# Pairing the third output tile of the six-block groups across groups, in an attention-and-MLP kernel with a written-out order

## The chip, the cores and the metric

The kernel runs on one core of one Trainium2 chip. The time is device microseconds from one launch of the whole program, the median of several runs. A core has TensorE (PE in the profile, with its weight loads as PEld), VectorE (DVE), ScalarE (ACT), GpSimd (POOL) and SyncE (SP), which here only issues DMAs. Each engine works through its own queue in order.

## The reference

Squared-ReLU attention, then an MLP with the quick GELU. Eight batches, 12 heads, 448 rows, head width 64; the MLP is 768 to 2048 to 768 on 3584 rows.

```python
scores = np.matmul(q, k.transpose(0, 1, 3, 2)) / np.sqrt(64)
attn = np.maximum(scores, 0.0) ** 2 / 448
x = np.matmul(attn, v).transpose(0, 2, 1, 3).reshape(8 * 448, 768)
h = x @ w_in
out = (h / (1.0 + np.exp(-1.702 * h))) @ w_out
```

All arrays are float32 in DRAM; the kernel multiplies in float16 and accumulates in float32.

## The kernel before, in words

**Attention** goes by units: a unit is four heads of one batch, 24 in all (three to a batch). k and q of a unit are loaded (by SP as float32 and cast on an engine, or by a POOL DMA that casts on the way), transposed (on PE for units 0 to 5, by a DMA on SP for the others), and multiplied in 7 steps of scores (line 150). Each step leaves two PSUM banks; relu (lines 161 and 163, on DVE or ACT) evicts each into an `at` tile, and square (L169 on ACT, or the helper tt, L88, on DVE or POOL) squares the tile in place. attn_v (L181) multiplies all seven `at` tiles of the unit with v, and xt_evac brings the result into `xe` or `xo`, the transposed input of the MLP.

**The MLP** goes by groups of 64-row blocks: `gblk = [6, 8] * 4`, so even groups have 384 rows and odd groups 512. Its first product is done for group 0 and half of group 1 plainly (m1, L228, word f), and for all others by Strassen's scheme in Winograd's form with seven products in place of eight (unit_product, word u, on weight differences winS and input differences T). The gelu on ACT goes into a `gf` tile of float32 (five buffers), and a "widening" on POOL (L217) scales it to float16 and writes it to the group's `ge` or `go` tile. Four words make up a unit's outputs there: t (snapshot of a PSUM bank), b (DVE adds the other bank to it), g (gelu), v (widening).

**The second product** (gelu times w_out, 768 columns in two halves of 384) goes by output tiles of 128 rows. An odd group has four such tiles, an even group three. Two tiles of a group (m and m+1) make a pair: seven products (pair_product, word p, eight matmuls each; L203 is the matmul helper that all of these share) on four sums of the gelu tile (a_sum, word A, DVE, tiles `as0` and `as1`, or in place) and on four differences of w_out (w_sum, word W). PSUM is evicted by h, l (L81, L85 and L396). An even group's third tile has no partner: in group 0 all three tiles are multiplied plainly (m2, word m, 16 matmuls for each half, evicted by n), in groups 2, 4 and 6 the third tile goes through single (word i, also 16 matmuls for each half, with one sum, n == 5).

**What sets the order.** The whole program is one list of words in a string. Each word is a function with its arguments, the engine after a colon and the PSUM banks after an at-sign: `s0.3@4.5` is scores of unit 0, step 3, into banks 4 and 5; `x0.3:p` squares on POOL; `p1.0.2` is product 2 of the pair (0, 1) of group 1. They are issued in this order, and every engine takes its own in it. The list was written by a planner that is not part of the kernel. A tile pool with n buffers makes the (n+1)th tile wait until an earlier one has been read.

Words used later: Lk, Lq (SP load), jk, jq (POOL load with cast), K, Q (cast), tk, tq (transpose on PE), ek, eq (its eviction), V (load of v), jwa, jwb (half of a w_in block), jo (a w_out block), S, T, W (Strassen differences of w_in, of the input, of w_out), z (dummy matmuls), o and q (stores, L328 and L334).

The start of the order before:

```python
"Lk0 z13@0 jk1 V1 jq1 I V0 K0:d tk0@1 z1 ek0 jk2 Lq0 Q0:a tq0@2 eq0 tk1@3 s0.3@4.5 "
```

Of the kernel before, what the change touches and what calls it, by code (L numbers as in the profile page):

```python
# [15 lines left out]
def kernel(  # L16
# [35 lines left out]
    for name, bufs in (("cst", 1), ("kst", 1), ("qst", 1), ("k16", 2), ("q16", 2), ("v16", 4),  # L52
                       ("kT", 3), ("qT", 3), ("at", 11), ("xe", 1), ("xo", 2),
                       ("T1", 1), ("T2", 1), ("T4", 1), ("ge", 1), ("go", 1), ("gf", 5),
                       ("as0", 1), ("as1", 1), ("osb", 3)):
        pool(name, bufs)
# [151 lines left out]
    def gt_of(g):  # L208
        if g not in gts:
            gts[g] = new("ge" if g % 2 == 0 else "go", [128, NF, 64 * gblk[g]], F16)  # L210
        return gts[g]

# [25 lines left out]
    def m1_widen(e, p, g, f):  # L238
        n = 64 * gblk[g]
        widen(e, gt_of(g)[:, f, 0:n], gfs.pop((g, f))[:, 0:n])  # L240
# [66 lines left out]
    def unit_widen(e, p, g, i, n):  # L307
        fh, th = unit_place[n]
        hn = 32 * gblk[g]
        f = WQ * i + 2 * fh  # L310
        widen(e, gt_of(g)[:, f:f + 2, th * hn:(th + 1) * hn],
              half_of(gfs.pop((g, i, unit_tile[n])), g).rearrange("p (t c) -> p t c", t=2))
# [9 lines left out]

    def store(e, p, g, m):
        t = osb.pop((g, m))
        for i in range(2):
            b, j = divmod(gcum[g] + 2 * m + i, J)
            r0 = b * S + j
            nc.sync.dma_start(out=out[r0:r0 + 63 * J + 1:J, :], in_=t[64 * i:64 * i + 64, :])  # L328

    def store_part(e, p, g, m, h, i):  # L330
        b, j = divmod(gcum[g] + 2 * m + i, J)
        r0 = b * S + j
        c = slice(h * NOUT, (h + 1) * NOUT)
        (nc.scalar if e == "a" else nc.sync).dma_start(  # L334
            out=out[r0:r0 + 63 * J + 1:J, c], in_=osb[g, m][64 * i:64 * i + 64, c])

    def m2(e, p, g, m, h):
        op[g, m, h] = bank(p, "op")
        mm(op[g, m, h][:, 0:NOUT], lambda f: gts[g][:, f, m * 128:(m + 1) * 128],
           lambda f: wout[h][f // WO][:, f % WO, :], NF, True)  # L340

    def m2_out(e, p, g, m, h):
        copy(e, out_tile(g, m)[:, h * NOUT:(h + 1) * NOUT], op.pop((g, m, h))[:, 0:NOUT], 1.0 / SC)
# [8 lines left out]
    def part(g, m, i):  # L352
        return gts[g][:, i * HF:(i + 1) * HF, m * 128:(m + 1) * 128]
# [3 lines left out]
    def a_sum(e, p, g, m, n):  # L357
        a11, a12 = part(g, m, 0), part(g, m, 1)
        if n == 5:
            sums[g, m, 5] = new(f"as{p.pop(0)}", [128, HF, 128], F16, "asum")  # L360
            tt(sums[g, m, 5], a11, a12, ALU.add, e)
            return
# [36 lines left out]
    def single(e, p, g, m, h):  # L399
        op[g, m, h] = bank(p, "os")  # L400
        o = op[g, m, h][:, 0:NOUT]
        a1, a2 = part(g, m, 0), part(g, m, 1)
        s, t = ((a1, wout[0][0]), (a2, wout[0][1])) if h == 0 else (
            (a1, wout[1][0]), (sums[g, m, 5], wout[1][1]))
        mm(o, lambda f: s[0][:, f, :], lambda f: s[1][:, f, :], HF, True)
        mm(o, lambda f: t[0][:, f, :], lambda f: t[1][:, f, :], HF, False)

# [15 lines left out]
    with tc.manual_schedule():  # L423
        two = {"S": s_sum, "W": w_sum, "T": t_sum, "s": scores, "r": relu, "x": square,
               "e": xt_evac, "f": m1, "m": m2, "o": store, "u": unit_product,
               "t": unit_snap, "b": unit_add, "A": a_sum, "p": pair_product, "h": pair_snap,
               "l": pair_last, "i": single, "n": m2_out, "q": store_part, "jo": load_w_out, "a": attn_v,
# [11 lines left out]
        home = {"K": "a", "Q": "p", "r": "a", "t": "a", "h": "a", "v": "p"}  # L439

        def do(word):
# [5 lines left out]
            if name in "gv":  # L447
                f = {"g": (m1_gelu, unit_gelu), "v": (m1_widen, unit_widen)}[name][len(args) - 2]
# [10 lines left out]
        def zeros(e, p, n):  # L459
# [8 lines left out]
            "Lk0 z13@0 jk1 V1 jq1 I V0 K0:d tk0@1 z1 ek0 jk2 Lq0 Q0:a tq0@2 eq0 tk1@3 s0.3@4.5 "  # L468
            "r0.3.1 jq2 ek1 s0.1@6.7 r0.1.0 r0.3.0:d s0.0@0.1 s0.2@2.3 tq1@5 r0.0.1:d r0.2.0 "
            "s0.5@4.6 r0.1.1 s0.4@1.2 r0.0.0 r0.5.1 s0.6@7.0 eq1 r0.4.0:d tk2@5 x0.0 s1.0@1.6 "  # L470
            "r0.4.1 x0.4 jwb2 r0.5.0 x0.5 r0.6.1 jk3 r0.2.1 r0.6.0 x0.3:p jq3 x0.1 ek2 r1.0.1 "
            "r1.0.0 x0.2 x0.6 s1.5@2.4 s1.2@0.3 r1.2.0 s1.1@7.6 r1.1.1 tq2@5 a0@1.0 r1.1.0 r1.5.0 "
            "s1.6@6.7 eq2 r1.2.1 x1.0 r1.5.1 r1.6.0 s1.3@5.2 r1.3.0 x1.1 x1.2 tk3@3 e0.0.0 "
            "e0.0.1:a jk4 x1.5 e0.1.0:a tq3@4 r1.3.1 ek3 eq3 jwb0 x1.3 jq4 jwa0 s1.4@6.5 r1.6.1 "
            "V2 x1.6 r1.4.1 r1.4.0 s2.0@1.3 s2.2@2.7 r2.2.1 e0.1.1:a s2.1@4.5 r2.0.1 r2.0.0 "
            "r2.2.0 tk4@6 r2.1.1 x1.4 a1@7.0 e1.0.1:a ek4 r2.1.0:d x2.2 s2.6@3.6 r2.6.0 tq4@1 "
            "r2.6.1 e1.0.0 s2.3@2.4 r2.3.0 e1.1.1 x2.0 x2.1 eq4 s2.4@5.0 r2.3.1 jwa1 s2.5@3.6 "
            "f0.2.0@2 r2.4.0 r2.4.1 jwb1 jwa2 jq5 f0.3.0@4 s3.0@1.5 x2.6 e1.1.0 x2.3 f0.3.1 x2.4 "
            "jk5 r2.5.0 r2.5.1 x2.5 r3.0.0:d S0.1 V3 f0.2.1 f0.0.0@7 f0.0.1 s3.1@0.3 r3.0.1 "
            "a2@6.5 jwb3 r3.1.1:d r3.1.0 s3.2@1.0 e2.0.0 f0.1.0@3 e2.0.1:a r3.2.1 r3.2.0 G3 "  # L480
            "e2.1.1:a e2.1.0 x3.0 f0.1.1 f0.1.2 g0.1 x3.1:p V4 f0.2.2 s3.5@6.0 r3.5.0:d g0.2 "
            "s3.4@1.5 f0.0.2 v0.1 f0.3.2 r3.4.0 V5 r3.4.1 f0.4.0@3 r3.5.1:d x3.2 x3.5 g0.3 g0.0 "
            "f0.4.1 s3.3@2.6 s3.6@1.0 jwa3 f0.8.0@5 r3.3.1 r3.6.0 v0.0 r3.3.0 f0.4.2 g0.4 f0.8.1 "
            "f0.8.2 s4.1@4.7 s4.3@6.1 r3.6.1:d s4.0@0.2 f0.6.0@3 f0.6.1 r4.1.0 r4.3.1 x3.6 V9 "
            "f0.6.2 r4.3.0 x3.3 f0.5.0@4 r4.1.1:d r4.0.1:d x3.4 f0.5.1 S0.2 x4.1 f0.5.2 v0.4 "
            "s4.2@7.1 x4.3 a3@2.6 g0.8 g0.5 r4.2.1:d s4.4@5.4 r4.2.0 r4.0.0 tq5@7 g0.6 v0.2 jo1.0 "
            "Lk6 r4.4.0:d r4.4.1 tk5@0 eq5 s4.5@1.3 s4.6@4.5 ek5 e3.0.1:a f0.11.0@6 x4.2:a "
            "f0.7.0@7 f0.11.1 f0.11.2 r4.6.1:d r4.5.0 r4.5.1:d r4.6.0:d f0.10.0@0 f0.10.1 f0.7.1 "
            "x4.6 e3.0.0:a jo0.0 x4.5:a x4.4 f0.10.2 S2.1 g0.11 s5.1@1.5 s5.0@2.3 x4.0:p v0.5 "
            "f0.7.2 v0.11 f0.14.0@4 r5.0.1:d v0.6 f0.14.1 g0.10 r5.1.0 r5.1.1 r5.0.0 f0.14.2 "  # L490
            "jo0.1 S1.1 g0.14 g0.7 s5.4@6.0 a4@1.3 s5.3@5.2 r5.4.0:d v0.7 r5.3.0 e4.0.0:a "
            "s5.2@4.7 r5.4.1:d r5.2.1:d f0.12.0@6 x5.0:p e4.0.1:a f0.13.0@0 r5.2.0:d f0.12.1 "
            "f0.12.2 x5.4:a g0.12 v0.3 f0.15.0@5 f0.15.1 s5.5@7.1 r5.5.1 s5.6@4.3 r5.3.1:d x5.3 "
            "r5.5.0:d r5.6.0:d f0.13.1 r5.6.1 jo1.1 f1.7.0@2 f0.13.2 f1.1.0@6 x5.1:p v0.12 v0.10 "
            "v0.14 K6:p x5.5:a g0.13 f0.15.2 f1.5.0@1 f1.5.1 f1.7.1 S2.2 S2.4 x5.2:a x5.6:a "
            "f0.9.0@7 f0.9.1 f0.9.2 f1.4.0@3 S2.3 g0.15 g0.9 a5@4.0 e5.0.1:a f1.0.0@5 f1.0.1 "
            "f1.3.0@7 f1.1.1 Lq6 Q6:a e5.0.0 T1.1 T1.2 S1.2 v0.13 f1.7.2 g1.7 f1.3.1 v1.7 v0.9 "
            "Lq7 f1.3.2 f1.4.1 f1.4.2 f1.5.2 Rk6 u1.2.0@0 f1.6.0@4 Rq6 S3.1 g1.5 f1.6.1 g1.3 "
            "f1.2.0@2 f1.0.2 f1.6.2 v1.3 v0.15 t1.2.0 S3.3 g1.0 v0.8 g1.6 v1.0 Lk7 T1.4 S3.2 g1.4 "
            "u1.2.2 S3.4 W2.1 f1.2.1 f1.2.2 S1.4 u1.3.0@1 v1.4 W1.1 Q7:a f1.1.2 g1.1 v1.5 v1.1 "  # L500
            "u1.2.1@7 b1.2.1 g1.2.1 v1.2.1 v1.6 m0.0.0@5 u1.2.3 g1.2 s6.2@4.3 T1.3 Lq8 t1.3.0 "
            "s6.1@6.2 u1.3.2 S0.3 t1.2.2 n0.0.0:a r6.2.0 u1.2.4 r6.1.1:d r6.2.1:d s6.0@5.4 r6.0.1 "
            "r6.0.0 x6.0:a t1.3.2 V11 t1.2.4:d W0.1 u1.3.1@2 W2.2 Rq7 W0.2 m0.0.1@3 K7:p Q8:a "
            "b1.3.1 b1.2.3 g1.2.3 Rk7 u1.2.5 u1.2.6 u1.3.4 r6.1.0 W3.1 S0.4 v1.2 V7 u1.3.3 g1.2.5 "
            "v1.2.3 s6.4@4.5 s6.3@6.0 S1.3 n0.0.1 t1.3.4 g1.3.1 b1.2.6 b1.3.3 s6.5@3.7 r6.4.0 "
            "u1.3.5 x6.1:p r6.3.0:d r6.4.1:d r6.5.0 W1.2 v1.3.1 v1.2.5 u1.3.6 Lk8 g1.3.5 W3.2 V6 "
            "x6.4:a r6.3.1:d x6.2:a r6.5.1 Rq8 b1.3.6 K8:p m0.1.0@4 s6.6@6.3 W2.4 v1.3.5 g1.3.3 "
            "v1.3.3 s7.2@5.1 g1.2.6 x6.3 W1.4 v1.2.6 Lq9 g1.3.6 s7.0@0.2 r7.2.1 r7.0.0 x6.5:a Q9 "
            "r6.6.1:d r7.2.0:d Lk9 r7.0.1 m0.1.1@7 r6.6.0:d n0.1.0:a Rk8 s7.1@3.1 x6.6 W3.4 "
            "x7.0:a a6@5.0 s7.3@6.2 r7.1.0:d r7.1.1 n0.1.1 Lq10 s7.4@4.3 x7.2 e6.0.1:a K9:p "  # L510
# [164 lines left out]
```

## Time and profile before

| What | Value |
|---|---|
| Median of 3 runs | 369.98 us (369.61 to 370.27) |
| The profiled execution's own time | 369.32 us |
| Its span, first to last instruction | 367.5 us |
| Busy: PE, DVE, ACT, POOL | 357.2, 290.2, 276.8, 179.0 us |
| Granted TensorE clock | 0.998 |
| DMA | 51.39 MB, mean 140 GB/s |

The page gives the busy time of each engine and its share of the span. Matmuls overlap and their ends are modelled, so that a busy PE is not PE at its peak. A row of a stage table holds the stretch, its length, then busy time and instruction count for PE, PEld, DVE, ACT and POOL, then the granted clock, the DMA share and GB/s. A row of a timeline holds start, duration, engine, line, operation, output and input with their shapes, the count of instructions that it merges, and in square brackets how long the engine was idle before and who ended that. In a row of groups the mean of one instruction is its duration, which with pipelining is longer than the step from one to the next.

### The profile page before, as it was taken

What the parts mean: (1) busy time and instruction counts of PE and PEld (TensorE: products, weight loads), DVE (VectorE), ACT (ScalarE), POOL (GpSimd) and SP (SyncE); (2) the same over time, 40 slices, a digit from 0 to 9 for tenths busy, and PEclk for the clock granted to TensorE, in tenths of its full rate; (3) what the DMA queues carried; (4) which work ended last, traced back from release to release, by engine and by line L of the source; (5) the groups of instructions that cost most, each with busy time, mean ns of one, the idle gap of its engine ahead of it and who ended that gap; (6) DMA issues with size and microseconds to landing.
All of it is one profiled execution on the core that took longest, in us unless ns stands there. A gap on an engine that the chain in (4) does not pass through costs nothing.

```text
span 367.5 us, 9086 instructions
## 1 busy us (share of the span) xinstructions
PE 357.2 (97%) x3570; PEld 231.1 (63%) x3570; DVE 290.2 (79%) x519; ACT 276.8 (75%) x542; POOL 179.0 (49%) x229
## 2 busy tenths in 40 slices
PE   7899999999999999999999999999999999999994
PEld 4454545664569555886559755786549755787662
DVE  3999968599997877878898788767887899755642
ACT  3998976687888998889958898878995897174310
POOL 6838695674115585256404856367342536043300
PEclk9999999999999999999999999999999999999999
DMA  9999999799964885978583396368943042300244
GB/s 197 195 205 204 241 209 219 129 172 207 130 179 118 165 236 98 204 164 186 102 167 73 98 199 136 102 146 162 239 98 77 0 112 28 87 0 2 70 114 119
DMA packets 65228, 51.39 MB, mean 140 GB/s; under 512 B 35745, under 2 KB 61857, under 8 KB 65185
## 3 DMA queue, kind: packets, MB, share of 16 engines
q1 hardware_dynamic: 48256, 36.32, 42.4%
q0 software_dynamic: 16608, 14.09, 25.5%
q8 instruction: 28, 0.46, 0.5%
q10 hardware_dynamic: 320, 0.39, 0.4%
q14 instruction: 16, 0.12, 0.1%
HBM read 45.61 MB, written 11.01 MB: 154 GB/s over the span
## 4 chain that ended last, share of the span: by engine, by line
PE 84%; DVE 10%; ACT 2%; DMA 1%; issue 1%; POOL 1%; SPq 0%; POOLq 0%; DVEq 0%; ACTq 0%
PE hx L203 29%; PE ox L203 26%; PE sc L150 9%; PE ht L228 7%; PE av L181 7%; PE os L203 4%; DVE at L88 3%; PE op L203 3%; DVE at L161 2%; ACT at L163 2%; DVE wT L88 1%; DMA qst<-in_q_dram 1%; DVE asum L88 1%; POOL ge L217 1%; POOL at L88 1%
## 5 line engine op out<-in xcount | busy, mean ns | idle before, releaser
L163 ACT ACTIVATE at<-sc 128x448 f16<-128x448 f32 x215 | 104.7, 567 | 13.2 <-PE sc L150 12.8
L161 DVE TENSOR_SCALAR at<-sc 128x448 f16<-128x448 f32 x121 | 71.8, 618 | 12.9 <-PE sc L150 12.5
L217 POOL TENSOR_SCALAR go<-gf 128x512 f16<-128x512 f32 x64 | 41.6, 650 | 64.0 <-ACT gf L214 47.2
L88 DVE TENSOR_TENSOR gf<-hx,gf 128x512 f32<-128x512 f32 (+1 forms) x78 | 47.9, 627 | 26.8 <-PE hx L203 14.2
L203 PEld LDWEIGHTS <-win 128*128 128x128 f16 x624 | 56.4, 98 | 8.4 <-issue 2.8
L88 POOL TENSOR_TENSOR at<-at 128x896 f16<-128x896 f16 x27 | 45.7, 1694 | 29.8 <-ACT at L163 18.0
L217 POOL TENSOR_SCALAR ge<-gf 128x384 f16<-128x384 f32 x64 | 35.8, 559 | 45.9 <-ACT gf L214 28.7
L169 ACT ACTIVATE at<-at 128x896 f16<-128x896 f16 x57 | 53.9, 955 | 0.9 <-DVE at L161 0.6
L150 PE MATMUL sc<-qT,kT 64*64 64x448 f16 x672 | 52.4, 359 | 2.2 <-DVE at L161 0.6
L88 DVE TENSOR_TENSOR at<-at 128x896 f16<-128x896 f16 x84 | 53.7, 673 | 0.8 <-ACT at L163 0.4
L214 ACT ACTIVATE gf<-gf 128x512 f32<-128x512 f32 (+1 forms) x78 | 43.2, 579 | 9.4 <-DVE gf L88 9.4
L203 PE MATMUL ox<-wout,go 128*128 128x384 f16 x256 | 46.5, 327 | 0.0
L203 PEld LDWEIGHTS <-winS 128*128 128x128 f16 x468 | 42.7, 98 | 4.5 <-issue 1.0
L203 PEld LDWEIGHTS <-go 128*128 128x128 f16 x320 | 29.9, 98 | 22.6 <-issue 4.8
L203 PEld LDWEIGHTS <-ge 128*128 128x128 f16 x288 | 27.5, 98 | 19.7 <-issue 3.3
L79 ACT ACTIVATE gf<-hx 128x512 f32<-128x512 f32 (+1 forms) x51 | 27.2, 543 | 15.3 <-PE hx L203 7.2
L203 PE MATMUL hx<-T,winS 128*128 128x256 f16 (+1 forms) x312 | 37.0, 261 | 0.0
L181 PE MATMUL av<-at,v 64*64 64x448 f16 x672 | 36.2, 350 | 0.6 <-DVE at L88 0.4
L150 PEld LDWEIGHTS <-kT 64*64 64x64 f16 x672 | 17.7, 105 | 27.9 <-issue 23.5
L203 PE MATMUL hx<-xo,win 128*128 128x256 f16 x252 | 32.1, 273 | 0.0
L203 PE MATMUL ox<-wT,asum 128*128 128x384 f16 x176 | 31.8, 327 | 0.0
L203 PEld LDWEIGHTS <-asum 128*128 128x128 f16 x200 | 18.7, 98 | 15.3 <-issue 3.1
(78 smaller groups left out, 481.6 us busy)
## 6 DMA issues: line engine op xcount, KB each, us to landing
out_dram<-osb SPq DMA_DIRECT2D x52, 192.0 KB, 3.3
kst<-in_k_dram SPq DMA_DIRECT2D x19, 448.0 KB, 5.2
qst<-in_q_dram SPq DMA_DIRECT2D x19, 448.0 KB, 4.2
v<-in_v_dram POOLq DMA_DIRECT2D x24, 224.0 KB, 5.4
win<-in_moe_w_in_dram POOLq DMA_DIRECT2D x8, 384.0 KB, 9.5
wout<-in_moe_w_out_dram POOLq DMA_DIRECT2D x4, 768.0 KB, 12.3
k<-in_k_dram POOLq DMA_DIRECT2D x5, 224.0 KB, 6.5
q<-in_q_dram POOLq DMA_DIRECT2D x5, 224.0 KB, 6.0
```

The source lines that it names most:

```text
L79: nc.scalar.activation(out=o, in_=i, func=AF.Copy)
L88: eng[e].tensor_tensor(out=o, in0=x, in1=y, op=op)
L150: nc.tensor.matmul(out=sc[a][c, 0:S], lhsT=st["kT"][r, j, c], rhs=st["qT"][r, :, c], start=True, stop=True)
L161: nc.vector.tensor_scalar(out=o, in0=i, scalar1=0.0, scalar2=None, op0=ALU.max)
L163: nc.scalar.activation(out=o, in_=i, func=AF.Relu)
L169: nc.scalar.activation(out=at, in_=at, func=AF.Square)
L181: nc.tensor.matmul(out=av[s][64 * a:64 * a + 64, 0:S], lhsT=v16[r, a, 64 * j:64 * j + 64], rhs=at[r, a, :], start=(j == 0), stop=(j == J - 1))
L203: nc.tensor.matmul(out=o, lhsT=lhs(i), rhs=rhs(i), start=start and i == 0, stop=i == n - 1, skip_group_check=True)
L214: nc.scalar.activation(out=o, in_=i, func=AF.Gelu_apprx_sigmoid, scale=1.0 / SC)
L217: eng[e].tensor_scalar(out=o, in0=i, scalar1=SC, scalar2=1.0, op0=ALU.mult, op1=ALU.mult)
L228: nc.tensor.matmul(out=hp[g, f][:, 0:n], lhsT=w[:, i, fo:fo + 128], rhs=xts[g][:, i, 0:n], start=i == 0, stop=i == NK - 1)
```

## The change

The third output tile of an even group is no longer written to the group's own gelu tile. `ge` holds 256 rows in place of 384, and the other 128 go to a tile of their own, `gh` (two buffers), by a second widening on POOL (word y, m1_hold and unit_hold). The third tiles of groups 0 and 2, and of groups 4 and 6, are then multiplied as a pair: for groups 2 and 6 the pair (2, 3) takes its first half from the group before (g − 2) and its second from the group itself. m2, single, m2_out and the sum n == 5 go. So all 28 output tiles are in 14 pairs; group 0's first two tiles are a pair too. To make room v16 has three buffers (four before) and at ten (eleven before). The order of the words is a new one throughout, of 2008 words in place of 1939.

```diff
-... ("v16", 4), ("at", 11), ("ge", 1), ("go", 1), ("gf", 5),
+... ("v16", 3), ("at", 10), ("ge", 1), ("go", 1), ("gh", 2), ("gf", 5),
...
-            gts[g] = new("ge" if g % 2 == 0 else "go", [128, NF, 64 * gblk[g]], F16)
+            gts[g] = new("ge", [128, NF, 256], F16) if g % 2 == 0 else new("go", [128, NF, 512], F16)
...
+    def hold_of(g):
+        if g not in holds:
+            holds[g] = new("gh", [128, NF, 128], F16)
+        return holds[g]
...
     def m1_widen(e, p, g, f):
-        n = 64 * gblk[g]
-        widen(e, gt_of(g)[:, f, 0:n], gfs.pop((g, f))[:, 0:n])
+        n = 256 if g % 2 == 0 else 512
+        widen(e, gt_of(g)[:, f, 0:n], gfs[g, f][:, 0:n])
+
+    def m1_hold(e, p, g, f):
+        widen(e, hold_of(g)[:, f, :], gfs[g, f][:, 256:384])
...
+        c = 64 if g % 2 == 0 and th else hn
+        widen(e, gt_of(g)[:, f:f + 2, th * hn:th * hn + c], unit_src(g, i, n)[:, :, 0:c])
+
+    def unit_hold(e, p, g, i, n):
+        f = WQ * i + 2 * unit_place[n][0]
+        widen(e, hold_of(g)[:, f:f + 2, :], unit_src(g, i, n)[:, :, 64:192])
...
+    def first_block(g, m):
+        if g % 2 == 0 and m >= 2:
+            return gcum[g - 2 if m == 2 else g] + 4
+        return gcum[g] + 2 * m
...
     def part(g, m, i):
+        if g % 2 == 0 and m >= 2:
+            return holds[g - 2 if m == 2 else g][:, i * HF:(i + 1) * HF, :]
         return gts[g][:, i * HF:(i + 1) * HF, m * 128:(m + 1) * 128]
```

The words that differ in number, before and after: p 77 and 98, A 47 and 56, h 33 and 42, l 44 and 56, m 6 and 0, i 6 and 0, n 12 and 0, y 0 and 40, z 2 and 4 (14 and 18 matmuls). Between engines: squares on DVE 84 and 98, on ACT 57 and 40, on POOL 27 and 30; relus on ACT 215 and 224, on DVE 121 and 112; casts of k and q on ACT 14 and 21, on POOL 22 and 15. The start of the new order, and its end from group 7's units on:

```diff
+"jk1 Lq0 Q0:a z13@0 Lk0 jk2 jq1 I V0 tq0@1 z2 tk1@2 K0:d z2 tk0@3 tk2@4 eq0 tq1@5 z1 "
+"ek0 ek2 jq2 eq1 s0.6@6.7 r0.6.1 ek1 r0.6.0 jwa1 V1 s0.2@1.3 s0.0@0.4 r0.0.1 r0.2.0:d "
...
+"h6.2.2:d g7.3.3 p6.2.4 h6.2.4 u7.3.6 t7.2.4:d b7.2.3 u7.2.5 b7.3.6 v7.3.3 u7.3.5 "
+"l6.2.3 g7.2.3 u7.2.6 g7.3.5 p7.0.0@5 p6.2.6 v7.2.3 b7.2.6 p6.2.5 g7.2.5 l6.2.6 o6.0 "
+"g7.3.6 v7.2.5 g7.2.6 l6.2.5:a v7.3.1 v7.3.6 v7.2.6 v7.3.5 h7.0.0 A7.0.1@1 A7.0.2@0 "
+"p7.0.1@1 p7.0.2 h7.0.2 l7.0.1 p7.0.3 A7.0.3 p7.0.4 o6.3 p7.2.0@3 o6.2 h7.0.4:d "
```

## The prediction

> **What bounds the kernel now.** I read the shares of busy time first, then the chain that ended last, then a table of stages, and last the timelines of the start and the end.
>
> ```profile
> PE 357.2 (97%) x3570; PEld 231.1 (63%) x3570; DVE 290.2 (79%) x519; ACT 276.8 (75%) x542; POOL 179.0 (49%) x229
> PE 84%; DVE 10%; ACT 2%; DMA 1%; issue 1%; POOL 1%; SPq 0%; POOLq 0%; DVEq 0%; ACTq 0%
> ```
>
> TensorE is 84% of the chain; VectorE (DVE) is the only other engine with a share. The table of stages (busy time of each engine, count in brackets) is cut where the first unit product of groups 1 to 7 starts and where the last matmul ends:
>
> ```profile
> 0.00:28.00 28.00, 23.99 (x342) 13.19 (x346) 22.33 (x44) 21.11 (x47) 17.41 (x28) 1.00 1.14 199
> 28.00:59.50 31.50, 31.31 (x310) 15.52 (x303) 28.23 (x48) 25.40 (x51) 22.98 (x28) 1.00 1.26 220
> 59.50:106.40 46.90, 45.83 (x414) 26.92 (x412) 40.70 (x70) 37.27 (x73) 23.52 (x30) 1.00 0.93 160
> 106.40:148.40 42.00, 42.00 (x454) 28.57 (x453) 34.19 (x66) 37.38 (x74) 23.38 (x28) 1.00 0.72 171
> 148.40:191.10 42.70, 42.40 (x417) 28.72 (x416) 36.60 (x66) 36.10 (x68) 17.66 (x23) 1.00 0.78 160
> 317.20:362.90 45.70, 45.67 (x337) 32.65 (x334) 24.95 (x41) 16.37 (x31) 9.88 (x16) 1.00 0.21 53
> ```
>
> From 28 us on PE looks full, but ends of matmuls are modelled, so I also count its work: from the chain's steps, 2.60 us for 16 matmuls of 384 columns (162.5 ns each), 0.65 for six of 256, 0.50 for six of 192, 1.32 for one attention-times-v, 0.19 for four scores. Summed over the order of words that is 335.7 us. PE's last matmul ends at 362.9, so 27.2 us are lost: 11.9 before 59.5, 4.8 in the next stage (46.9 for 42.1 of work), 10.5 in all that follows. The first loss is a start in which DVE and ACT work without a pause:
>
> ```profile
> 1.26 0.92 POOL L104 DMA_DIRECT2D k<-in_k_dram  x1 [0.81 <-POOLq L659]
> 4.26 0.63 DVE L83 CAST k<-kst 128x896 f16<-128x896 f32 x1 [3.16 <-DMA kst<-in_k_dram]
> 7.74 0.95 PE L150 MATMUL sc<-qT,kT 64*64 64x448 f16 x16 [0.33 <-DVE qT L83]
> 8.20 9.28 ACT L163 ACTIVATE at<-sc 128x448 f16<-128x448 f32 x21 [1.81 <-PE sc L150]
> ```
>
> **What the Trainium skill says.** "TensorE: Matmul & The Clock Gate", section "Wait — 56ns, not 53.3ns?": a warm matmul takes its columns at 2.4 GHz plus 2.5 ns; for 384 columns 162.5 ns, exactly the trace's step. "SBUF — State Buffer", section "Who interferes with whom": DVE instructions with two SBUF inputs and GpSimd instructions that read SBUF lock each other out. The trace agrees: wT subtractions take 0.54 us at best and 1.88 us at 79.55, while POOL casts a k block (80.07 to 81.01).
>
> ```profile
> 74.10 0.55 DVE L88 TENSOR_TENSOR wT<-wout,wout 128x768 f16<-128x768 f16 x1
> 79.55 1.88 DVE L88 TENSOR_TENSOR wT<-wout,wT 128x768 f16<-128x768 f16 x1
> ```
>
> **The change part by part.** The sum is made on the profiled execution: 369.32 us, a span of 367.5 and 1.8 around it; the median of the runs is 369.98, so I carry the difference over to that.
>
> *Matmuls.* Before: 77 pair products of 8 matmuls, 6 calls of m2 and 6 of single of 16 each, 808. After: 14 pairs of 7 products of 8, 784. 24 fewer at 162.5 ns: **−3.9 us**, all on PE. Four more dummy matmuls stand where PE waits for data at the start: 0.
>
> *Sums and evictions.* Twelve of the new pairs' sums come, three of the singles' go: 9 × 0.70 (asum rows) = 6.3 us on DVE. Ten more DVE evictions × 0.55 = 5.5. The order moves 14 squares to DVE (14 × 0.64 = 9.0) and 9 relus away (−5.3); one evacuation of a snap goes too (−0.6). DVE +14.9, to about 305, 84% of the span. ACT: −17 squares × 0.95, +9 relus × 0.49, +7 casts × 0.95: −5. No row has the split widenings; 512 columns take 650 ns and 384 take 559, which makes 468 for 256 and 377 for 128 (estimates on that line). 40 extra instructions: +11.5 us on POOL, 3 squares more, 7 casts fewer: +10, to 189 of 364, covered as long as gf's five buffers last; a late hold keeps one and then ACT's next gelu, with all relus queued behind it, waits (bounds 0 and one widening, 0.5 us, taken 0). v16's fourth buffer and at's eleventh go: the order before holds 11 only twice, 0.
>
> *The start.* The new order puts tk1 ahead of K0 in PE's queue, and K0's cast takes the k16 buffer that tk1 must have read: two buffers, jk1 and jk2 both already out. jk1 is issued at 1.26 and the cast loads of this stretch land in 5.1 us at best: 6.4. Then tk1 0.6, K0 0.63, tk0 0.58, its eviction 0.62 behind q's: 9.0; PE first does tk2 and tq1, to 9.6. Behind K0 on DVE stand both evictions and its first relus, so PE and ACT wait for it too. First scores at 9.6 in place of 7.74, first relu on ACT at 9.9 in place of 8.2. DVE begins its relus 2.6 us later, at 10.8, but has two more evictions (1.2) behind it: 1.4 late. Up to a2 (26.7 before) its queue is also longer: 6 relus more, one S, one eviction and 2 squares fewer, +3.6 −0.7 −0.6 −1.3 = +1.0. So a2 at 29.1, with PE work ahead of it 17.2 (16.9 before): 2.1 more lost. From a2 to the first unit 31.4 us of PE work at the old pace (32.8 for 30.6) give 33.6: the mark is at 62.7 with 48.6 us done, 14.1 lost in place of 11.9. **+2.2**; bounds 0 (PE catches up: from 28 us the old order still lost 1.4 by 40) and 3.7 (ACT's 1.7 with both 1.0s).
>
> *Groups 0 and 1 (59.5 to 106.4).* Group 0's 96 plain matmuls needed no sums. Now its pair needs the wT differences and its own sums early: the words of this stage hold 49.6 us of DVE work for 45.3, at the stage's ratio of traced to listed time (40.7/45.3) +3.9, for 43.2 of PE work (42.1). DVE would be busy 44.6 of 48.1, 93%. In the old 80 to 107 it ran at 99% and PE lost 4.0. I take **+1.0**, between 0 and 3.9.
>
> *Later attention stretches.* From a12 to the units of group 4 the words hold 22.6 of DVE for 18.5 of PE (before 19.2 for 18.1), from a18 to group 6's 19.1 for 16.1 (19.3 for 18.5). At the traced ratios DVE is over PE by 1.6 and 0.7. Half can run on into the units that follow, where DVE has room: **+1.2**, between 0 and 2.3. Other stages shift work between them and add nothing.
>
> *The end.*
>
> ```profile
> 339.95 0.82 PE L203 MATMUL hx<-T,win 128*128 128x256 f16 x6
> 341.54 3.40 POOL L217 TENSOR_SCALAR go<-gf 128x512 f16<-128x512 f32 x5 [1.91 <-ACT gf L214]
> 345.77 0.69 DVE L88 TENSOR_TENSOR asum<-asum,go 128x1024 f16<-128x1024 f16 x1
> 345.80 1.47 PE L203 MATMUL ox<-wout,go 128*128 128x384 f16 x8
> ```
>
> Between the last unit product (over at 340.6) and group 7's second product PE now has 5.2 us of old work, and widenings and sums are done 5.85 after that product, before the third product needs them. The new order leaves three products there, 3.9: with one product more, 5.2 against 5.85. **+0.6**, between 0 and 1.3. The last evictions and stores stay as they are, 4.6 us.
>
> *SP and the loads.* SP's waits stand ahead of stores and loads that are early; nothing of PE's idle time is put down to SP's loads after 24 us. The loads that POOL issues move too, and group 0's pair needs wout earlier: 10.4 MB stand up to the last wout block in the new order, which the page's GB/s (9.6 MB by 46 us, 11.5 by 55) bring by 50 us, and the pair's first product comes after 43 us of PE work with 14 lost, at 57. At 0, with 7 us of cover.
>
> Sum: −3.9 + 2.2 + 1.0 + 1.2 + 0.6 = +1.1: profiled 370.4, median **371.1**.
>
> **The rivals.**
> *The saving arrives (faster).* One mechanism: PE is behind DVE's and ACT's start only until 40 us, and the ordinary loss after that (10.5 us of 246) holds room to catch up. For it: the 0.99 filling of 317 to 345. Against it: PE is already at 95 to 97% of its counted work from 40 to 80. Price: the three middle terms at 0, the end's 0.6 left: 369.98 − 3.9 + 0.6 = 366.7. It decides where start, groups 0 and 1 and the later stretches together cost under 3.3.
> *DVE becomes the bound.* More POOL reads and more two-input DVE work lock each other out, as at 79.55. For it: six of eight stages get more DVE work. Against it: 79% today. With these terms near their upper ends (+3.7, +2.5, +1.7, +0.6): 374.6.
> *It does not shorten the path.* The removed matmuls of group 0 stood where PE lost time anyway, so their 40 × 0.1625 = 6.5 us turn into idle time and only the rest counts, while the start costs half: about 370. Against it: later groups took over the deferred tile, and PE is full there.
>
> **How the numbers follow.** Forecast's case 0.54 (own range 369.3 to 373.2; slower 0.44, same 0.08, faster 0.02), saving arrives 0.26, DVE the bound 0.10, no shorter path 0.10 (same 0.08, faster 0.02). Within 0.2% (369.24 to 370.72) is what a measurement here can't tell from no change. Faster 0.30, same 0.16, slower 0.54. The range goes from the saving in full to the DVE case, 366.6 to 374.6, and leaves out about 0.17.
>
> **What would show it.** Right: 784 output matmuls; first scores near 9.6 us and first unit of group 1 near 62.7; DVE over 90% busy from there to group 2's units; DVE near 305 in all. Wrong: group 1's units at 60.5 or earlier, or group 2's before 108, would mean the saving arrived; asum or wT rows over 0.8 us on average mean the lock; PE idle on POOL's widenings in the even groups means that the holds cost what I put at nothing.

## The result, and the profile after

The changed kernel takes **382.35 us** (median of 4 runs, 381.93 to 385.93) against 370.12 for the kernel before on the same chip (369.61 to 370.81): ratio 1.035, interval 1.0286 to 1.0415. It is slower, as I forecast, but by 12 us and not by 1, and above the range. The profiled execution took 382.63 us with a span of 380.9.

The page's busy times and the engines' shares of the chain that ended last:

```profile
PE 361.1 (95%) x3550; PEld 230.8 (61%) x3550; DVE 311.0 (82%) x542; ACT 274.2 (72%) x541; POOL 193.9 (51%) x265
PE 62%; DVE 14%; POOL 10%; ACT 10%; issue 3%; POOLq 0%; DVEq 0%; ACTq 0%
```

PE has 20 matmuls fewer (24 gone, 4 dummies more) and is still busy for 4 us more, so part of its waiting must lie inside what counts as busy. Its share of the chain falls from 84% to 62%, and three other engines take over. The stages of the kernel after, cut as before (stretch, length, then busy time and count of PE, PEld, DVE, ACT, POOL):

```profile
0.00:64.20 64.20, 59.81 (x654) 30.76 (x655) 51.19 (x98) 48.34 (x98) 43.63 (x71) 1.00 1.17 202
64.20:112.50 48.30, 46.67 (x422) 26.61 (x421) 44.26 (x76) 41.97 (x84) 28.14 (x28) 1.00 0.84 186
112.50:150.40 37.90, 36.48 (x406) 24.91 (x405) 33.78 (x60) 32.22 (x68) 19.99 (x30) 1.00 0.75 143
150.40:197.80 47.40, 44.43 (x433) 29.47 (x432) 42.36 (x70) 35.38 (x70) 25.77 (x30) 1.00 0.60 137
...
238.90:285.80 46.90, 43.99 (x426) 29.12 (x424) 40.77 (x68) 35.22 (x68) 28.52 (x31) 1.00 0.73 145
...
328.20:375.90 47.70, 47.37 (x346) 33.48 (x343) 29.18 (x49) 16.50 (x31) 10.36 (x17) 1.00 0.22 61
```

The table below sets all stages side by side, with two experiments that are told further on. "Column work" is the columns of the recorded matmuls at the 2.4 GHz that the prediction took (a 64 by 64 tile counts a quarter, a 128 by 64 tile a half), each matmul in the stage in which it starts: a lower bound of what PE needs.

| Stage, up to the first unit product of | before | after | e6 (no POOL reads for squares) | e18 (147 matmuls fewer) | column work before, after |
|---|---|---|---|---|---|
| group 1 | 59.4 | 64.2 | 63.7 | 62.7 | 44.7, 45.7 |
| group 2 | 46.9 | 48.3 | 46.5 | 48.3 | 41.3, 42.6 |
| group 3 | 42.1 | 37.9 | 37.4 | 37.9 | 39.5, 32.6 |
| group 4 | 42.7 | 47.4 | 45.1 | 46.7 | 39.4, 41.0 |
| group 5 | 42.6 | 41.1 | 41.1 | 41.1 | 39.6, 38.1 |
| group 6 | 42.3 | 46.9 | 44.7 | 47.3 | 39.7, 39.8 |
| group 7 | 41.1 | 42.4 | 41.0 | 42.5 | 38.5, 38.3 |
| last matmul | 45.8 | 47.7 | 47.6 | 47.4 | 44.7, 46.1 |
| end | 4.6 | 5.0 | 5.0 | 4.8 | |
| sum | 367.5 | 380.9 | 372.1 | 378.7 | 327.4, 324.2 |

The 3.2 us that PE has less to do (24 matmuls gone, 4 dummies come) are there. But what it loses beside its work grows from 40.1 us (367.5 − 327.4) to 56.7 (380.9 − 324.2). Three stages lose most: that up to group 1's units, and those of groups 3 and 5 (rows "group 4" and "group 6"), both +4.6 or +4.7. The row "group 3" has 6.9 us less to do and is only 4.2 shorter.

The start went as I had traced it. First the load of jk1 lets tk1 run, then DVE casts K0, then the first scores and the first relu on ACT:

```profile
7.07 0.58 PE L131 MATMUL tr<-ident,k 128*64 128x128 f16 x14
7.69 0.63 DVE L83 CAST k<-kst 128x896 f16<-128x896 f32 x1 [6.59 <-PE tr L131]
9.94 2.28 PE L150 MATMUL sc<-qT,kT 64*64 64x448 f16 x24
10.37 1.85 ACT L163 ACTIVATE at<-sc 128x448 f16<-128x448 f32 x4 [5.19 <-PE sc L150]
```

The new thing is in DVE's rows. Before, squares took 673 ns and asum from asum and go 684 ns on average:

```profile
L88 DVE TENSOR_TENSOR at<-at 128x896 f16<-128x896 f16 x84 | 53.7, 673 | 0.8 <-ACT at L163 0.4
L88 DVE TENSOR_TENSOR asum<-asum,go 128x1024 f16<-128x1024 f16 x8 | 5.5, 684 | 0.1
```

After:

```profile
L88 DVE TENSOR_TENSOR at<-at 128x896 f16<-128x896 f16 x98 | 68.7, 737 | 0.7
L88 DVE TENSOR_TENSOR asum<-go 128x1024 f16<-128x1024 f16 x8 | 7.3, 917 | 0.9 <-POOL go L224 0.8
L88 DVE TENSOR_TENSOR asum<-asum,go 128x1024 f16<-128x1024 f16 x8 | 6.9, 869 | 0.1
...
L88 DVE TENSOR_TENSOR asum<-asum,ge 128x1024 f16<-128x1024 f16 x4 | 4.3, 1085 | 0.0
```

All rows with two inputs from SBUF hold 147.9 us (214 instructions, mean 691 ns) in place of 124.7 (191, 653 ns). The timeline shows one such place in the stage of group 5's units:

```profile
266.01 1.39 POOL L83 CAST q<-qst 128x896 f16<-128x896 f32 x1
266.64 1.30 DVE L88 TENSOR_TENSOR go<-go 128x1024 f16<-128x1024 f16 x1
267.37 2.12 POOL L88 TENSOR_TENSOR at<-at 128x896 f16<-128x896 f16 x1
267.87 2.16 DVE L88 TENSOR_TENSOR asum<-asum,go 128x1024 f16<-128x1024 f16 x1
...
270.62 0.57 PE L150 MATMUL sc<-qT,kT 64*64 64x448 f16 x8 [1.16 <-DVE at L161]
```

A cast on POOL takes 1.39 in place of about 0.95, two DVE sums 1.30 and 2.16 in place of 0.68, a POOL square 2.12 in place of 1.7: each overlaps one of the other engine. Behind the two sums on DVE is the relu for which PE then waits 1.16 us.

### The profile page after: what moved, and what is told of

It is laid out like the page before. It is cut to its first block, busy times and chain, and to the rows that moved or that the text cites. A ratio compares the mean times of both kernels' runs of the same rounds, so it can differ in the third digit from the quotient of the medians.

```text
span 380.9 us, 9109 instructions
## 1 busy us (share of the span) xinstructions
PE 361.1 (95%) x3550; PEld 230.8 (61%) x3550; DVE 311.0 (82%) x542; ACT 274.2 (72%) x541; POOL 193.9 (51%) x265
## 4 chain that ended last, share of the span: by engine, by line
PE 62%; DVE 14%; POOL 10%; ACT 10%; issue 3%; POOLq 0%; DVEq 0%; ACTq 0%
PE ox L203 25%; PE hx L203 19%; PE sc L150 6%; PE av L181 5%; DVE at L88 5%; ACT at L163 5%; PE ht L235 4%; POOL ge L224 3%; POOL go L224 3%; DVE asum L88 3%; DVE at L161 3%; ACT gf L221 2%; POOL gh L224 2%; PE zp L467 1%; DVE osb L408 1%
## 5 line engine op out<-in xcount | busy, mean ns | idle before, releaser
L163 ACT ACTIVATE at<-sc 128x448 f16<-128x448 f32 x224 | 109.6, 561 | 19.5 <-PE sc L150 19.1
L88 POOL TENSOR_TENSOR at<-at 128x896 f16<-128x896 f16 x30 | 52.8, 1763 | 50.6 <-ACT at L163 22.0
L161 DVE TENSOR_SCALAR at<-sc 128x448 f16<-128x448 f32 x112 | 66.1, 614 | 10.9 <-PE sc L150 8.4
L88 DVE TENSOR_TENSOR at<-at 128x896 f16<-128x896 f16 x98 | 68.7, 737 | 0.7
L224 POOL TENSOR_SCALAR go<-gf 128x512 f16<-128x512 f32 x64 | 44.4, 694 | 47.3 <-ACT gf L221 44.0
L150 PE MATMUL sc<-qT,kT 64*64 64x448 f16 x672 | 54.5, 359 | 3.1 <-DVE at L161 1.3
L203 PE MATMUL ox<-wout,go 128*128 128x384 f16 x256 | 46.2, 326 | 0.1
L203 PE MATMUL ox<-wT,asum 128*128 128x384 f16 x224 | 40.6, 327 | 3.7 <-DVE asum L88 2.4
L224 POOL TENSOR_SCALAR ge<-gf 128x384 f16<-128x384 f32 (+2 forms) x64 | 28.9, 452 | 29.6 <-ACT gf L221 25.8
L169 ACT ACTIVATE at<-at 128x896 f16<-128x896 f16 x40 | 38.1, 961 | 0.7 <-DVE at L161 0.5
L81 ACT ACTIVATE osb<-ox 128x384 f32<-128x384 f32 x34 | 16.6, 491 | 22.4 <-PE ox L203 22.2
## 6 DMA issues: line engine op xcount, KB each, us to landing
wout<-in_moe_w_out_dram POOLq DMA_DIRECT2D x4, 768.0 KB, 20.1
```

Of the source, the lines that this page charges most:

```text
L81: nc.scalar.activation(out=o, in_=i, func=AF.Copy, scale=scale)
L88: eng[e].tensor_tensor(out=o, in0=x, in1=y, op=op)
L150: nc.tensor.matmul(out=sc[a][c, 0:S], lhsT=st["kT"][r, j, c], rhs=st["qT"][r, :, c], start=True, stop=True)
L161: nc.vector.tensor_scalar(out=o, in0=i, scalar1=0.0, scalar2=None, op0=ALU.max)
L163: nc.scalar.activation(out=o, in_=i, func=AF.Relu)
L169: nc.scalar.activation(out=at, in_=at, func=AF.Square)
```

## The experiments

Each experiment is compared with the kernel before on the same chip (369.2 to 370.3 us there, so that medians of two experiments can differ by 1 us for that alone). My theory T1 was the lock, the mutual blocking that the prediction describes: more two-input rows on DVE and more POOL reads hold each other up, and PE waits. The rivals were R1, the places of the new order; R2, the 40 holds on POOL; and R4, POOL's time itself.

### First round: engines, holds, and POOL's squares

e1 gave squares, relus and casts back to the engines of the order before (without a letter a square is on DVE, a relu on ACT, Q on POOL):

```diff
-x1.0:p ... x2.2:a ... r2.4.0:d ... Q22:a
+x1.0 ... x2.2 ... r2.4.0 ... Q22
```

> The new order word for word, but each square, relu and cast runs on the engine that the order before gave it (17 squares go back from DVE and POOL to ACT, 7 casts from ACT to POOL, 9 relus from ACT to DVE). Theory T1 (more two-input work on DVE together with more POOL reads lock each other out; that stretches DVE by some 10 us, and PE waits for it): a good part of the 12 us above the time before comes back, 375 to 378 us. Rival R1 (the new order's places make the waits, whichever engine does the work): the old engines don't fit the new places, 381 us or more. Rival R2 (the 40 holds on POOL, which I put at nothing): 381 to 383, for they stay, and POOL gets seven casts on top.

**429.4 us** (1.159). A miss for T1's number, and R1's "381 or more" holds. This order, written out for one set of engines, doesn't bear another set: ACT's relus wait 46.2 us for scores (19.1 in the changed kernel). So large a loss tells nothing on the lock.

e2 made the holds narrow:

```diff
-        widen(e, hold_of(g)[:, f:f + 2, :], unit_src(g, i, n)[:, :, 64:192])
+        widen(e, hold_of(g)[:, f:f + 2, 0:8], unit_src(g, i, n)[:, :, 64:72])
```

> The changed kernel, but each of the 40 holds (y) writes 8 columns of each tile in place of 128; the rest of the hold tile is set to zero once (two to four memsets on DVE), so the third tiles' values are left out. The instructions and their order stay. R2 (the holds' POOL time is what costs): POOL falls by 8 to 15 us and the time to 373 to 376. T1 (lock): the holds are a small part of POOL's reads, 379 to 381. R1 (order): 380 to 382.4.

**385.0 us.** The holds' rows fell from 17.0 to 11.2 us on POOL and nothing was won. The memsets that fill the tile cost something of their own (POOL waits 6.9 us for them), so this excludes R2's 6 to 9 us, not a small cost.

e3 and e4 took the SBUF reads out of POOL's squares, in the new kernel and in the old:

```diff
+        elif e == "p":
+            nc.gpsimd.memset(at, 0.5)
```

> The changed kernel, with the 30 squares on POOL replaced by memsets of the same tile (POOL writes and reads nothing from SBUF; these squares are left out of the computation). T1: asum rows fall from 0.9 to under 0.75 us mean, DVE from 311 to about 302, and the time by 5 to 8 us to 374 to 377, clearly more than the same edit gives in the kernel before. R1 (order): under 2 us, as in the kernel before. R2 (holds): 2 to 4 us, because POOL has room again, with DVE's rows shorter or not.

> The kernel before, with its 27 squares on POOL replaced by memsets of the same tile (squares left out of the computation). All theories: little to gain where PE is 97% busy, 368 to 370 us; what the new kernel gains beyond this under the same edit is the lock's or POOL's share in the slowdown.

**373.4 us** (1.0086, 1.0064 to 1.0107) in the new kernel, **368.95** (0.9986, 0.9963 to 1.001) in the old. The same edit is worth 9 us in one order and 0.5 in the other, where the interval includes no change. But a memset (0.84 us) is also half as long as a square (1.76), so that R4 would say the same.

### Second round: the lock against POOL's time, and the start

e6 kept POOL as long but without reads, e7 kept one read and was short:

```diff
         elif e == "p":
-            tt(at, at, at, ALU.mult, e)          (square)
+            nc.gpsimd.memset(at, 0.5)            (e6: twice)
+            nc.gpsimd.memset(at, 0.5)
+            nc.gpsimd.tensor_copy(out=at, in_=at)   (e7)
```

> The changed kernel with each of the 30 squares on POOL replaced by two memsets of the same tile, 2 x 0.84 = 1.69 us, about as long as the square (1.76) but with no read from SBUF (these squares are left out of the computation). Theory T1 (DVE's two-input rows and POOL's reads lock each other out): 373 to 375 us, asum rows at 0.73 and DVE's squares at 0.67 us mean, as with one memset. Rival R4 (it is POOL's own time, at tiles that come 0.9 us later and widenings queued behind): 380 to 382.4.

> The changed kernel with each of the 30 squares on POOL replaced by a copy of the tile onto itself: one SBUF read in place of two (these squares are left out of the computation). T1: the lock is still there for as long as the copy lasts; if it lasts about 1 us, 376 to 379 us, with DVE's squares at 0.69 to 0.71 us mean. R4 (POOL's time): 373 to 375, as with one memset, for the copy is nearly as short.

e6: **375.6 us** (four runs, two at 373 to 374 and two at 377 to 378; 1.0179, interval 1.0114 to 1.0245; the profiled execution 373.84). POOL and DVE groups of e6:

```profile
L171 POOL MEMSET at<- 128x896 f16 x30 | 25.4, 845 | 44.8 <-ACT at L163 29.6 <-DVE at L161 10.3 <-DVE q L83 4.5
L172 POOL MEMSET at<- 128x896 f16 x30 | 25.4, 845 | 1.7
```

```profile
L88 DVE TENSOR_TENSOR at<-at 128x896 f16<-128x896 f16 x98 | 61.1, 659 | 0.8
L88 DVE TENSOR_TENSOR asum<-go 128x1024 f16<-128x1024 f16 x8 | 5.6, 704 | 0.9 <-POOL go L227 0.8
L88 DVE TENSOR_TENSOR asum<-asum,go 128x1024 f16<-128x1024 f16 x8 | 5.5, 683 | 0.1
```

POOL is nearly as busy as in the changed kernel (190.3 us for 193.9), the two memsets last about as long as a square (1.69 us for 1.76), and the time falls by 6.8 us (spans: 8.8). DVE's two-input rows fall from 147.9 to 135.6 us, DVE in all from 311.0 to 299.2. R4, which asked for 380 or more, is out as the main cause: the read is what costs. What e3 gains beyond e6 (2.2 us by the medians, 0.8 by the spans) may be POOL's time. e7 (**376.8 us**, T1's 376 to 379 and not R4's 373 to 375; its copies last 1.01 us) has DVE's squares at 688 ns, between 659 and 737: a copy reads too, for a shorter time. "SBUF — State Buffer", section "Who interferes with whom", in the Trainium skill says that a two-input DVE instruction contends with a GpSimd instruction that reads SBUF, "not with one that only writes it"; e6 agrees, with 659 ns against 737.

The table shows where: the 8.8 us are 1.8, 0.5, 2.3, 2.2 and 1.4 in five of the stages with attention, 0.5 up to group 1, and nearly nothing elsewhere. The lock is not all of the slowdown: e6's span is still 4.6 us over the kernel before (4.3 of them up to the first unit of group 1), although PE has 3.2 us less to do.

e5 and e11 put the start of the order before ahead of the new order. e11 kept all of the old words in their places:

```diff
-jk1 Lq0 Q0:a z13@0 Lk0 jk2 jq1 I V0 tq0@1 z2 tk1@2 K0:d z2 tk0@3 ...
+Lk0 z13@0 jk1 V1 jq1 I V0 K0:d tk0@1 z1 ek0 jk2 Lq0 Q0:a tq0@2 ...   (105 words)
```

> The new order from its 106th word on, behind the first 105 words of the order before (K0 ahead of tk1, first scores at 7.7 us); words that one of the two lacks are left out or put at the seam. If the start costs what the marks show (first unit of group 1 at 64.2 in place of 59.4 us) and later stages don't give it back: 377.5 to 378.5 us. If DVE's stretch behind it swallows the lead: 380 to 382.

> The new order behind the first 105 words of the order before, now with all of these words kept in their places (in the first try ek3 had been left for the seam, and PE waited 2.67 us for it at 21.4 us). If the start of the new order costs what the marks show, the first unit of group 1 comes at 60.5 to 62 in place of 64.2 us and the time is 378.5 to 380.5; if the rest of the stage (DVE's queue behind the start) sets it, the mark stays at 63 to 64 and the time at 381 to 382.5.

e5: **384.5 us**, spoiled by the seam as the second expectation says. e11: **382.0 us** (1.0327), and the first unit of group 1 comes at 64.2 us, where it was, though the first scores come at 7.75. The lead is lost by 33 us. Time and mark are close to the expectation's second case, but that DVE's queue sets them is not shown. In e11's timeline PE then waits for a w_in block:

```profile
32.68 1.47 PE L235 MATMUL ht<-xe,win 128*128 128x384 f16 x8 [1.15 <-DMA win<-in_moe_w_in_dram]
```

e8 moved POOL's squares to ACT:

```diff
-x1.0:p ... x2.1:p ... x3.4:p ...
+x1.0:a ... x2.1:a ... x3.4:a ...
```

> The changed kernel with the 30 squares of POOL on ACT in the same places (0.95 us each, +28 us on ACT, to about 302). T1: DVE falls by 8 to 10 us to about 302 and the rows of asum to 0.73; ACT at 80% takes some of it back: 374 to 379 us. R1 (the order's places are what costs, each engine's queue being planned): 382 or more.

**386.7 us.** DVE fell to 299.7 us, as in e6, but ACT rose to 297.2 us and from 10% to 19% of the chain. T1's time was wrong, its DVE right; the time is the one that R1 had given. With the squares on ACT the wait seems to change engine, and e8 alone doesn't decide between T1 and R1.

### Third round: places, buffers, and the pair by itself

e12 cleared words of other work out of group 5's units:

```diff
-... Lq22 v5.1.1 ... Q22:a V19 ... V18 ... V20 ... (and x18.3:p)
+e17.0.1:a V18 V19 V20 ... g5.0.5 Q22:a v5.0.5 ... b5.3.6 x18.3:p
```

> The changed kernel with four words moved out of group 5's units: V18 to V20 (three DMA issues of 0.76 us on POOL) ahead of them, the POOL square x18.3 behind them, and ACT's cast Q22, which waits 2.38 us for its DMA, five ACT words later. R1 (words of other work stand ahead of widenings and gelus in POOL's and ACT's queues): the stage of these units falls from 46.9 to 44.5 to 45.5 us, the time by 1.4 to 2.4 to 380 to 381. T1 (lock only): 46.5 to 47, 382.

**383.6 us**, the stage 48.5 in place of 46.9. R1 in this form is wrong: these words at these places are not what costs.

e9 paired only two third tiles, in the old order; e10 was its control with the same smaller buffers:

```diff
-("v16", 4), ("at", 11)          i4.2.0 i4.2.1  ...  i6.2.0 i6.2.1
+("v16", 3), ("at", 10)          y4.0.3 ... y4.3.6  ...  A6.2.1 A6.2.2 p6.2.0 ... p6.2.6
```

> The pairing by itself, for two tiles: the kernel before with its old order and engines, but the third tile of group 4 held in a gh tile (8 widenings more on POOL) and multiplied with that of group 6 as a pair of 56 matmuls in place of 64 (8 fewer x 162.5 ns = 1.3 us), all in the last stage, with two sums and six evictions more on DVE and ACT where they have room; v16 with 3 buffers and at with 10, loads of v put in the order of need. If pairing brings its matmuls where DVE has room: 1.3 us under the time of the next kernel (the same buffers without a pair), and 0.5 to 1.3 us under the time before. If the pair costs what its sums and holds take (R2): the time before or up to 2 us over it.

> The kernel before with v16 at 3 buffers and at at 10, loads of v in the order of need and moved behind the attn_v that frees their buffer, nothing else. I put the loss of these buffers at nothing: within 0.5 us of the time before. If the tighter buffers are part of the slowdown: 1 to 4 us over it.

e10: **375.4 us**, e9: **379.4 us**; both are above every range given. e10 is no measure of the buffers: my moved loads of v stand at places where POOL waits for them, as e10's waits show (before, the longest two groups of these were 6.0 and 2.5 us):

```profile
POOL v L104 <- PE sc L150: 31.0, 8, 7.2
...
POOL v L104 <- PE av L181: 7.2, 2, 4.6
```

As a control it serves. Against it, e9 takes 32 matmuls (5.2 us) out of the stage of group 5's units and gains 1.9 in that stage and the one before it (43.9 and 41.5 us against 43.5 and 43.8), adds 24 (3.9 us) to the last stage and pays 5.7 (51.5 against 45.8). The pair with its sums, holds and evictions, eight matmuls fewer, made the kernel 4 us slower. That was the first sign that a matmul is not worth its duration here.

e13 took only at's eleventh buffer from the old kernel; e14 gave both buffers back to the new one, e15 gave gf seven:

```diff
-("at", 11)                                  +("at", 10)                       (e13)
-("v16", 3), ("at", 10), ("gh", 2)           +("v16", 4), ("at", 11), ("gh", 1)   (e14)
-("gh", 2), ("gf", 5)                        +("gh", 1), ("gf", 7)             (e15)
```

> The kernel before with at at 10 buffers in place of 11, nothing else. I put this loss at nothing because the old order holds 11 only twice. If that holds: 369.3 to 370.5 us. If each relu that takes a new tile now waits for an attn_v one tile earlier all along, 372 to 375 us.

> The changed kernel with the buffers of before given back: at 11, v16 4. The room comes from one gh tile in place of two: group 2's holds overwrite those of group 0, and group 6's those of group 4 (the third tiles of groups 0 and 4 are left out). If the smaller buffers cost the new order time (by e10 up to 5 us): 377 to 380 us, with the first unit of group 1 before 63. If the new order was planned to live with them: 381 to 383.

> The changed kernel with one shared gh tile as in the run with big buffers (the third tiles of groups 0 and 4 left out), the room given to gf: 7 buffers in place of 5. If gelus that wait for a gf buffer, with relus behind them, are what is left beside the lock (0.7 to 0.9 us waits of PE on ACT gf in group 5's units, at 40 to 43 us in group 0): 378 to 380.5. If not: 381.5 to 383.

e13: **369.45 us** (0.9997, 0.9981 to 1.0013): nothing, as I had put it. e14: **382.6**: nothing. e15: **379.65** (1.0288): gf's five buffers cost the new order 2.7 us by the medians (every run of e15 is below every run of the changed kernel), 1.1 of it in the stage of group 5's units. I had put them at nothing as long as they last; they don't last.

### Last: what a matmul is worth

e16 and e18 leave most matmuls of some second products out, in the old and in the new kernel:

```diff
-               lambda f: wout[h][f // WO][:, f % WO, :], NF, True)     (e16: m2; single likewise)
+               lambda f: wout[h][f // WO][:, f % WO, :], 2, True)
...
-        mm(op[g, m, c][:, 0:NOUT], lambda f: a[:, f, :], lambda f: w[:, f, :], HF,   (e18)
+        k = 1 if g == 0 or (g, m) in ((2, 2), (6, 2)) else HF
+        mm(op[g, m, c][:, 0:NOUT], lambda f: a[:, f, :], lambda f: w[:, f, :], k,
```

> What a matmul taken away is worth in the kernel before: of the 16 matmuls of each plain second product (m and i words, 12 of them) only 2 are done, 168 fewer in all (these products are left out), and nothing else changes. At 162.5 ns each, 27.3 us: 13.65 in the stage of group 1's units, 4.55 each in those of groups 3, 5 and 7. If PE's work is the path everywhere, as I summed: 342 to 345 us. If in the stretches with attention these products fill time in which PE would wait for DVE and ACT (the third rival): a half or less of that in the first three stages, 351 to 360 us, and about 4 in the last stage.

> What a matmul taken away is worth in the changed kernel: of the eight matmuls of each product of the three pairs that the change adds (groups 0, 2 and 6, p0.0, p2.2, p6.2) only one is done, 147 fewer (these products are left out), all else stays. At 162.5 ns each they are 23.9 us: 358 to 360 if PE's work is the path. If PE's work fills time that the others set, as in the kernel before (where 27.3 us of it gave 3.5): 376 to 380.

e16: **366.2 us** (0.9913), slower than both cases of the expectation. 27.3 us of matmuls gave 3.4 us. Its first stage, in which no word was changed, took 2.8 us longer (see the last section); from there on 5.6 us came of 27.3: 3.3 of 13.65 in the stage of group 1's units, 0.2 of 4.55 in that of group 3's, 1.1 of 4.55 in that of group 5's, and 1.1 of 4.55 in the last. In the first of these PE is busy for 36.43 us, where it was 45.83:

```profile
62.20:106.00 43.80, 36.43 (x330) 20.33 (x329) 39.54 (x69) 37.17 (x73) 23.57 (x30) 0.96 0.89 169
```

e18: **380.8 us** (1.0276, interval 1.0231 to 1.032). This is close to the expectation's second case: 23.9 us of matmuls gave 1.5 us by the medians, 2.2 by the spans. Of the 2.2, 1.5 lie up to the first unit of group 1, where only 7 matmuls (1.1 us) are gone; the other 140 (22.8 us) gave 0.7. Six of the seven products of group 0's pair lie in the stage of group 1's units; 42 matmuls are gone there, 6.8 us, and the stage takes 48.3 us as ever. The last stage, PE busy for 47.37 of 47.70 us, lost 49 matmuls, 8.0 us, and is 0.3 shorter. The row of this stage in e18 and PE's timeline there show what takes their place:

```profile
326.50:373.90 47.40, 42.13 (x296) 28.98 (x294) 28.92 (x49) 16.47 (x31) 10.36 (x17) 0.96 0.22 61
```

```profile
342.89 0.81 PE L203 MATMUL hx<-xo,win 128*128 128x256 f16 x6 [0.68 <-DVE gf L83]
...
346.29 0.82 PE L203 MATMUL hx<-xo,win 128*128 128x256 f16 x6 [1.60 <-ACT gf L79]
...
355.00 0.50 PE L203 MATMUL ox<-wout,go 128*128 128x384 f16 x2 [1.52 <-POOL go L224]
356.45 4.45 PE L203 MATMUL ox<-wT,asum 128*128 128x384 f16 x16 [0.95 <-DVE asum L88]
360.74 2.76 PE L203 MATMUL ox<-wout,go 128*128 128x384 f16 x16
```

In the changed kernel PE waits for 0.3 us in this stage, so these waits (0.68, 1.60, 1.52, 0.95) were covered by the matmuls that are gone. After the last two, 16 matmuls take 4.45 us in place of 2.76 and the stage's granted clock is 0.96, so that 1.7 us went to a slower PE.

e17 tried what e13 and e15 point to, as a complete kernel:

```diff
-("at", 11), ... ("gf", 5)
+("at", 10), ... ("gf", 6)
```

> The kernel before, complete, with at at 10 in place of 11 (which cost nothing in the run before) and gf at 6 buffers in place of 5, in the room that this leaves. The new kernel gained 2.7 us from two more gf buffers. If the old order's gelus wait for gf too (ACT gf waits 2.6 and 2.1 us in all for POOL's widenings): 368.5 to 369.3. If its order keeps clear of that: the time before, 369.3 to 370.

**370.0 us** (1.0001, 0.9981 to 1.002): the old order keeps clear of gf's limit. No complete version beat the kernel before.

## Why the prediction was wrong

Two steps failed. The larger is the lock between DVE's two-input rows and POOL's reads: the sum put it at nothing, and the runs show 6.8 to 9.0 us. The other is the term of the matmuls, which took PE's work for the time. That the time rose, as forecast, is in part luck: most of the rise comes from what the sum did not hold.

*The matmuls, −3.9 us.* This step failed in its mechanism. "24 fewer at 162.5 ns: −3.9 us, all on PE" takes PE's work for the path because PE is 97% busy and has 84% of the chain. e18 prices 147 matmuls of the added pairs at 1.5 to 2.2 us of 23.9, under 0.1 of their duration; e16 gives 0.1 to 0.2 in the old kernel. Both prices hold some time at a slower clock, which 24 matmuls fewer need not bring; but at a clock of 1.00, 42 matmuls fewer (6.8 us) gave nothing in e18's stage of group 1's units and 0.7 in that of group 3's. At one such price for all, 24 matmuls bring 0.2 to 0.8 us, and the term was 3.1 to 3.7 too good. That is an estimate: priced apart, the 192 plain ones that go at e16's worth and the 168 that come at e18's, the exchange would bring 1.4 to 4.7. So it is shown that the time does not follow PE's work, and open how much of the 3.9 was lost. My third rival had this mechanism, but for group 0 alone; against it I wrote that in later groups "PE is full there". A full PE was no evidence: in e18's last stage 8.0 us of a full PE's work made way for waits and a slower clock. In the kernel before I had even counted 27 us in which PE does no work, and seen DVE and ACT without a pause up to 28 us.

*DVE's work, and the lock.* I forecast DVE at about 305 us; it came to 311.0. The work I had listed was right in kind, but each row was priced at the mean length of the kernel before. The missing term is that POOL's squares, and a cast in the timeline above, lengthen the two-input rows that they meet, and are lengthened by them: 12.3 us on DVE's rows between the kernel after and e6, whose DVE total is 299.2. In time the squares' reads are 6.8 us (e6, medians) to 9.0 (e3, where POOL's time falls too) in the new order and 0.5 in the old: what the lock costs depends on the order. "DVE becomes the bound" was the right rival, and "asum rows over 0.8" its right sign (0.92, 0.87 and 1.09 us in three groups of them); wT rows, named beside it, gave none (0.65 us, and 0.84 already before). But I had set "79% today" against it and priced it from the ends of my own terms: 374.6.

*Groups 0 and 1, +1.0.* The stage took 1.4 us more, DVE 92% busy where I had said 93%. e6's stage is 0.4 shorter than before, so the lock made this difference and the count of the words did not.

*The start, +2.2.* First scores at 9.94 (9.6 forecast), a2 at 29.06 (29.1), the mark at 64.2 (62.7). The steps up to a2 were right, what they set was not: e11 starts as before and reaches the same mark, and its time is the same. So the +4.8 of this stage seems to come from the words after the first 105, as far as one execution of each can tell (see the last section). Of these gf's buffers are no part (64.8 in e15), nor is the lock much (63.7 in e6); which wait it is stays open.

*Later stretches, +1.2, and POOL's costs at nothing.* The stages of groups 3 and 5 took 4.7 and 4.6 more, of which the lock is 2.3 and 2.2, and gf's buffers 0.9 and 1.1 by e15. I had bounded gf's part by one widening, 0.5 us, and taken 0; e15 gives 2.7 in all. Not all of this can be added up, for the same waits may be counted in two runs. The holds' width was rightly put at nothing (no gain in e2), and so were at's and v16's buffers (e13, e14). The words of other work in POOL's and ACT's queues, which I suspected after the result, were not it either where e12 moved them. The loads of wout landed later, after 20.1 us in the median in place of 12.3, and no wait of PE names them, as put.

*The end, +0.6.* The last stage took 1.9 more for 1.4 more column work; the end 0.4 more.

Together: 371.1, plus 6 to 9 for the lock, is 377 to 380; the matmuls add up to 3.7 and gf's buffers up to 2.7; measured are 382.35. That is consistent, but no more: these were measured one at a time, and the sum leans on the other terms' sum of 5.0, which came out of other places than I said.

## What to carry to other kernels

In a kernel whose order is written out for four engines, a busy PE at 97% need not mean that a matmul less is a matmul gained: leave some out first and see what the time does. When a change moves element-wise work with two SBUF inputs to DVE or gives POOL more to read, price the rows by what they take when they meet, and look for pairs of long rows in the timeline. An order is planned for its engines: moving work back to where it was (e1, e8) or putting another start ahead of it (e5, e11) didn't undo one part of such a change.

## What I had not expected of the hardware

In e16 and e10 the first stage took 62.2 and 62.0 us in place of 59.4, though their first words are the old order's. In e16 tk1 starts at 7.30 us in place of 6.86 and waits for its load, and the next two loads that PE waits for are 0.8 us later. e13, on the same chip as e16, has 59.4. It may be the execution and not the kernel: e17's profiled execution, the slowest of its 14 (372.35 us, the others from 369.14), has a first stage of 62.7, and its later stages are those of the kernel before. What moves these landings was not settled; differences of 2 to 3 us in the first stage alone should not be read as an edit's effect.

PE's clock: in the stage of group 1's units of e16 the granted clock was 0.96, where the kernel before has 1.00, so that part of the work taken from PE was paid back as a slower clock. It was also 0.66 between 25 and 30 us in e16 and between 20 and 25 us in e17, which belongs to their longer first stages; in e10 it is 1.00 there, so it is not the whole reason.
